# Keys of the first batch on a second DMA queue: windowed attention followed by a leaky-ReLU layer

## The chip, the cores and the metric

The kernel runs on one core of a Trainium2 chip. The metric is device time in microseconds, as the median of several runs. The core has five engines with instruction streams of their own, which meet only at semaphores: TensorE (PE, matrix products; loading its weights is listed as PEld), VectorE (DVE), ScalarE (ACT), GpSimd (POOL) and SyncE (SP). Memory transfers are done by 16 DMA engines. An engine that issues a transfer puts it into its queue and goes on; here SP and POOL issue transfers.

## The reference

Attention with a window of 32 positions on each side, over 8 batches, 8 heads, 576 positions and 64 channels, and after it two matrix products with a leaky ReLU between them:

```python
scores = scale * np.matmul(q, k.transpose(0, 1, 3, 2))
mask = np.abs(pos[:, None] - pos[None, :]) <= 32
scores = np.where(mask, scores, -1e9)
attn = softmax(scores)                      # over the last axis
attn_out = np.matmul(attn, v)
x = attn_out.transpose(0, 2, 1, 3).reshape(4608, 512)
h = x @ w_in                                # 512 -> 2048
out = np.maximum(0.01 * h, h) @ w_out       # 2048 -> 512
```

All inputs and the output are float32; the kernel computes in bfloat16 with float32 sums.

## The kernel before

Heads are handled in pairs (`p` from 0 to 3), so that two heads of 64 channels fill 128 partitions. A step of the attention is one half of the positions (288) of one pair of one batch; there are 64 of them. Step `i` has four parts. `score` (L270) multiplies keys and queries into `ps`, takes the exponential on ACT into `e` (L280), and multiplies it by a 0/1 mask on POOL into `prob` (L282). `sums` (L295) forms the row sums with a matrix of ones and their reciprocal on DVE (L309). `product` (L312) multiplies by the values into `x`. `scaled` (L332) multiplies `x` by the reciprocals into `xT` (L334). When the four pairs of a half are done, `h_tile` (L360, matmuls at L348) and `o_tile` (L381, matmuls at L390) do the dense layers for these 288 positions, and ACT applies the leaky ReLU (L355).

The order of the instructions is written out by hand and each engine takes its own in that order. The change lies in the opening, before a steady mixture of attention steps and dense matmuls begins.

The opening does this. At the top SP issues the loads of batch 0 in this order: queries and keys of pair 0, of pair 1, values of pair 0 (two halves, L91), queries and keys of pairs 2 and 3 (L79), values of pairs 1 to 3. A query or key load is 96 partitions x 2 heads of 1536 bytes each, 288 KB; a half of a value load is 64 partitions x 9 runs of 256 bytes, 144 KB. Eight completion counters are handed round over these loads, so a ninth load is issued only when the first has landed.

Queries are cast to bfloat16 on DVE (the last pair's on ACT, L195), keys on POOL (L197). TensorE transposes both (L225), ACT copies the transposes out of the accumulators (L233 for queries, L239 for keys), and DVE places keys into `kbd` (L258), a tile that holds the two heads on the diagonal and zeros elsewhere. Values go into a similar tile, `vbd`: pair 0 by POOL (`cast_v`, L205), pairs 1 to 3 by ACT (L203). The zeros in `kbd` and `vbd` are written once at the beginning: `kbd[0]` by DVE (L134), `vbd[0]` for pairs 0 to 2 by ACT (`clear`, L125 to L129, called at L135 to L137) and for pair 3 by POOL (L158).

POOL's order in the opening matters below. After the masks: keys of pair 0, keys of pair 1, both value halves of pair 0, the masking of step 0, keys of pair 2, the masking of step 1, keys of pair 3, three of the four loads of `w_in` (L448, issued from POOL since these loads also convert the type), the masking of step 2, the fourth load of `w_in`, then further maskings with the four loads of `w_out` (L452) between them. TensorE's filler matmuls (`keep_busy`, L398) add nothing to the result.

DVE's order is: query casts of pairs 0 and 1, key placement of pair 0, of pair 1, query cast of pair 2, reciprocal of step 0, key placement of pair 2, `xT` of step 0, reciprocal of step 1, key placement of pair 3, reciprocal of step 2, and so on. `first_pair` (L456) emits the transposes of one pair's queries and keys and the key placement.

Of the kernel before, what the change touches and what calls it, by code (L numbers as in the profile page):

```python
# [16 lines left out]
def kernel(  # L17
# [14 lines left out]
    nc = tc.nc  # L32
# [30 lines left out]
    qf, kf, vf = {}, {}, {}  # L63
    RUN = S // 96
# [3 lines left out]
    def load_qk(b, p, behind=None):  # L68

        for into, src, name in ((qf, q, "qf"), (kf, k, "kf")):
            t = fload.tile([96, 2, RUN * D], FP32, name=f"{name}{p}")
            if behind is not None:
                behind.memset(t[0:1, 0, 0:1], 0.0)
                behind = None
            heads = src[b, 2 * p:2 * p + 2]
            if b < BY_DMA:
                nc.sync.dma_start(out=t, in_=heads.rearrange("a (p c) d -> p a (c d)", c=RUN))  # L79
            else:  # L80
                nc.sync.dma_start(
                    out=t.rearrange("p a (g e) -> p a g e", g=3),
                    in_=heads.rearrange("a (g p c) d -> p a g (c d)", g=3, c=2),
                )
            into[b, p] = t

    def load_v(b, p):
# [7 lines left out]
        vf[b, p] = t  # L95

    load_qk(0, 0)
    load_qk(0, 1)
    load_v(0, 0)
    load_qk(0, 2)  # L100
    load_qk(0, 3)
    for p in range(1, NPAIR):
# [18 lines left out]
    vbd = [const.tile([128, NPAIR, NB, 128], BF16, name=f"vbd{i}") for i in range(2)]  # L121
# [3 lines left out]
    def clear(t, p):  # L125
        flat = t[:, p].rearrange("p n j -> p (n j)")
        nc.scalar.activation(
            out=flat, in_=zero.to_broadcast([128, NB * 128]), func=AF.Copy,
        )  # L129
# [4 lines left out]
    nc.vector.memset(kbd[0], 0.0)  # L134
    clear(vbd[0], 0)  # L135
    clear(vbd[0], 1)
    clear(vbd[0], 2)  # L137

# [7 lines left out]
    for lo in (0, 64):  # L148
        w = win[lo:lo + 64]
        nc.gpsimd.affine_select(  # L150
            out=w, in_=w, compare_op=ALU.is_ge, fill=0.0,
# [3 lines left out]
            out=w, in_=w, compare_op=ALU.is_ge, fill=0.0,  # L155
# [5 lines left out]
    def make_mask(hf):  # L161
# [12 lines left out]
        out=ps[:, 512:512 + HALF], in_=zero.to_broadcast([128, HALF]), func=AF.Copy,  # L174
# [11 lines left out]
    def cast_qk(b, p, q_eng=None):  # L186
        for eng, src, dst in ((q_eng or nc.gpsimd, qf, qb), (nc.gpsimd, kf, kb)):
            if b < BY_DMA:
                parts = [(dst[:, p], src[b, p].rearrange("p a (c d) -> p c a d", d=D))]
            else:  # L190
                by_c = src[b, p].rearrange("p a (g c d) -> c p g a d", g=3, c=2)
                parts = [(dst[:, p, 3 * c:3 * c + 3], by_c[c]) for c in range(2)]
            for to, tok in parts:
                if eng is nc.scalar:
                    eng.activation(out=to, in_=tok, func=AF.Copy)  # L195
                else:
                    eng.tensor_copy(out=to, in_=tok)  # L197

    def cast_v(b, p, on_act=False):
        for a in range(2):  # L200
            r = slice(64 * a, 64 * a + 64)
            if on_act:
                nc.scalar.activation(out=vbd[b % 2][r, p, :, r], in_=vf[b, p][r], func=AF.Copy)  # L203
            else:
                nc.gpsimd.tensor_copy(out=vbd[b % 2][r, p, :, r], in_=vf[b, p][r])  # L205
# [42 lines left out]
    def place_keys():  # L248

        while landing and landing[0][0] <= state["done"]:  # L250
            unplaced.append(landing.pop(0)[1:])
        while unplaced:
            b, p, kT = unplaced.pop(0)
            for a in range(2):
                r = slice(64 * a, 64 * a + 64)
                to = kbd[b % 2][r, p, :, r]
                if b < BY_DMA:
                    nc.vector.tensor_copy(out=to, in_=kT[r].rearrange("p (n j) -> p n j", j=64))  # L258
                else:
                    nc.vector.tensor_copy(  # L260
                        out=to.rearrange("p n (m c) -> p n c m", c=2),
                        in_=kT[r].rearrange("p (c n m) -> p n c m", c=2, n=NB),
                    )
# [192 lines left out]
    def first_pair():  # L456
        next(first)
        next(first)
        place_keys()
# [2 lines left out]
    make_mask(0)  # L462
    cast_qk(0, 1, nc.vector)
    first_pair()
    first_pair()
    cast_v(0, 0)
    score(0)
# [112 lines left out]
    at, t = {}, 0.0  # L580
# [66 lines left out]
```

## Time and profile before

| | |
|---|---|
| median of 3 runs | 319.5 us (319.1 to 320.05) |
| span of the profiled execution, first to last instruction | 318.5 us |
| time of the profiled execution beside its span | not listed |
| granted TensorE clock, mean | 1.000 |
| PE busy | 303.2 us, 95% |
| DVE busy | 218.2 us, 69% |
| POOL busy | 191.6 us, 60% |
| ACT busy | 182.6 us, 57% |
| bytes moved by DMA | 49.46 MB, mean 155 GB/s |

The profile comes from one execution of the kernel. Times in it are counted in microseconds from the first instruction. Its page has the busy share of each engine, the span in 40 equal slices with a digit for each (9 is 90% busy or more), the chain of work that ended last, and groups of instructions by line. The trace behind it can be asked for a timeline (start, duration, engine, line, operation, result and source, shapes, and in brackets the idle time before it with what ended it), for the waits, and for the DMA queues in a window of time. In the queue views q1 holds what SP issues and q0 what POOL issues. `SPq` is SP's issuing of a transfer; a DMA's landing is when its completion is seen.

### The profile page before, as it was taken

How to read it: one execution, taken by the hardware profiler on the slowest of the kernel's cores; microseconds unless marked ns; L12 is line 12 of the kernel's file. 1: busy time of each engine (PE TensorE's matmuls, PEld its weight loads, DVE VectorE, ACT ScalarE, POOL GpSimd, SP SyncE). 2: the span in 40 equal slices, each digit the busy share in tenths (PEclk: the TensorE clock that was granted, in tenths of full speed). 3: DMA queues.
4: the chain of work that ended last, by engine and by line, in shares of the span. 5: the costliest groups of instructions: out<-in, count | busy, mean ns of one | idle time of the engine just before them, and what ended most of it. 6: DMA issues, size and time to landing. Idle time of an engine off the chain costs nothing.

```text
span 318.5 us, 6474 instructions
## 1 busy us (share of the span) xinstructions
PE 303.2 (95%) x2449; PEld 204.3 (64%) x2449; DVE 218.2 (69%) x259; ACT 182.6 (57%) x393; POOL 191.6 (60%) x251
## 2 busy tenths in 40 slices
PE   2679998999999999999999999999999999999996
PEld 1467774585765858576765858576665858576653
DVE  5678955869655997688755997688745988565100
ACT  7577698474652828374652828375552837464531
POOL 7798963974546866686546866586637866330000
PEclk9999999999999999999999999999999999999999
DMA  8999999997999995399735995399733430000101
GB/s 179 211 186 218 267 250 203 250 206 181 216 242 196 231 206 150 82 251 203 155 76 127 238 227 136 75 223 232 162 76 104 109 70 33 35 35 2 66 31 71
DMA packets 108400, 49.46 MB, mean 155 GB/s; under 512 B 68816, under 2 KB 103888, under 8 KB 108368
## 3 DMA queue, kind: packets, MB, share of 16 engines
q1 hardware_dynamic: 104144, 44.84, 66.8%
q0 software_dynamic: 4224, 4.19, 8.0%
q8 instruction: 19, 0.31, 0.4%
q14 instruction: 13, 0.11, 0.1%
HBM read 36.70 MB, written 9.44 MB: 145 GB/s over the span
## 4 chain that ended last, share of the span: by engine, by line
PE 89%; DMA 3%; DVE 2%; SPq 1%; POOL 1%; ACT 1%; issue 1%; DVEq 0%; ACTq 0%
PE mm L348 39%; PE mm L390 38%; PE x L320 5%; PE ps L275 4%; DMA kf<-in_k_dram 3%; PE s L301 2%; DVE r L309 2%; SPq L79 1%; POOL w_in_bf L448 1%; DVE xT L334 1%; PE tp L225 1%; PE s L304 1%; ACT vbd L203 0%; SPq L91 0%; POOL prob L282 0%
## 5 line engine op out<-in xcount | busy, mean ns | idle before, releaser
L309 DVE RECIPROCAL r<-s 128x288 f32<-128x288 f32 x64 | 125.2, 1956 | 56.5 <-PE s L301 53.3
L282 POOL TENSOR_TENSOR prob<-e,mask 128x576 bf16<-128x576 bf16 x64 | 81.5, 1274 | 87.8 <-ACT e L280 41.1
L348 PE MATMUL mm<-xT,w_in_bf 128*128 128x288 bf16 x1024 | 134.0, 286 | 0.3
L390 PE MATMUL mm<-w_out_bf,gT 128*128 128x512 bf16 (+2 forms) x592 | 130.4, 373 | 0.2 <-DMA w_out_bf<-in_moe_w_out_dram 0.2
L355 ACT ACTIVATE gT<-mm 128x288 bf16<-128x288 f32 x256 | 101.4, 412 | 24.8 <-PE mm L348 8.5
L348 PEld LDWEIGHTS <-w_in_bf 128*128 128x128 bf16 x1024 | 98.4, 98 | 24.8 <-issue 0.6
L390 PEld LDWEIGHTS <-gT 128*128 128x128 bf16 x592 | 56.3, 98 | 59.6 <-issue 0.3
L395 ACT ACTIVATE o_sb<-mm 128x512 f32<-128x512 f32 (+2 forms) x37 | 21.7, 586 | 92.0 <-PE mm L390 92.0
L280 ACT ACTIVATE e<-ps 128x576 bf16<-128x576 f32 x64 | 41.4, 648 | 9.4 <-PE ps L275 9.2
L197 POOL CAST kb<-kf 96x384 bf16<-96x384 f32 (+1 forms) x56 | 35.5, 656 | 4.6 <-DMA kf<-in_k_dram 4.6
L205 POOL CAST vbd<-vf 64x576 bf16<-64x576 f32 x50 | 34.5, 689 | 1.8 <-DMA vf<-in_v_dram 0.4
L334 DVE TENSOR_TENSOR xT<-x,r 128x288 bf16<-128x288 f32 x64 | 29.3, 458 | 8.2 <-PE x L320 1.2
L260 DVE COPY kbd<-kT 64x576 bf16<-64x576 bf16 x48 | 32.3, 672 | 0.3
L275 PE MATMUL ps<-qT,kbd 128*128 128x128 bf16 (+2 forms) x320 | 26.5, 215 | 1.8 <-DVE kbd L258 1.2
L275 PEld LDWEIGHTS <-kbd 128*128 128x128 bf16 x320 | 21.0, 100 | 10.6 <-DVE kbd L258 1.5
L320 PE MATMUL x<-prob,vbd 128*128 128x128 bf16 (+2 forms) x320 | 26.0, 213 | 1.3 <-ACT vbd L203 0.7
L197 POOL CAST qb<-qf 96x384 bf16<-96x384 f32 x48 | 24.5, 538 | 0.0
L320 PEld LDWEIGHTS <-vbd 128*128 128x128 bf16 x320 | 20.6, 99 | 3.9 <-ACT vbd L203 1.8
L292 DVE TENSOR_TENSOR both<-prob 128x288 bf16<-128x288 bf16 x52 | 19.7, 380 | 0.9
L301 PE MATMUL s<-both,ones_bd 128*128 128x288 bf16 x52 | 14.9, 286 | 0.0
L258 DVE COPY kbd<-kT 64x576 bf16<-64x576 bf16 x16 | 7.1, 444 | 8.7 <-ACT kT L239 8.6
L225 PE MATMUL tp<-ident,qb 96*128 96x96 bf16 x48 | 4.4, 243 | 6.2 <-DVE qb L197 6.2
(43 smaller groups left out, 86.6 us busy)
## 6 DMA issues: line engine op xcount, KB each, us to landing
qf<-in_q_dram SPq DMA_DIRECT2D x32, 288.0 KB, 4.5
kf<-in_k_dram SPq DMA_DIRECT2D x32, 288.0 KB, 5.0
vf<-in_v_dram SPq DMA_DIRECT2D x64, 144.0 KB, 4.2
out_dram<-o_sb SPq DMA_DIRECT2D x35, 256.0 KB, 3.6
w_in_bf<-in_moe_w_in_dram POOLq DMA_DIRECT2D x4, 512.0 KB, 8.6
w_out_bf<-in_moe_w_out_dram POOLq DMA_DIRECT2D x4, 512.0 KB, 16.8
qT<-qb SPq DMA_TRANSPOSE x24, 4.1
kT<-kb SPq DMA_TRANSPOSE x24, 3.2
```

The costliest lines, as they stand in the source:

```text
L197: eng.tensor_copy(out=to, in_=tok)
L205: nc.gpsimd.tensor_copy(out=vbd[b % 2][r, p, :, r], in_=vf[b, p][r])
L260: nc.vector.tensor_copy(out=to.rearrange("p n (m c) -> p n c m", c=2), in_=kT[r].rearrange("p (c n m) -> p n c m", c=2, n=NB),)
L275: nc.tensor.matmul(ps_v[:, n_, :, i0:i0 + n], kbd[b % 2][:, p, blk], by_c[:, :, hf * EVEN + i0:hf * EVEN + i0 + n], start=True, stop=True,)
L280: nc.scalar.activation(out=e, in_=ps[:, P0:P0 + 2 * HALF], func=AF.Exp, scale=scale)
L282: nc.gpsimd.tensor_mul(pr.rearrange("p n c i -> p (n c i)"), e, mask[hf].rearrange("p n c i -> p (n c i)"),)
L309: nc.vector.reciprocal(r, s)
L320: nc.tensor.matmul(x_v[:, :, i0:i0 + n], vbd[b % 2][:, p, blk, :], pr[:, n_, :, i0:i0 + n], start=(blk == parts[0][1]), stop=(blk == parts ...
L334: nc.vector.tensor_mul(place(i), x, r)
L348: nc.tensor.matmul(h[:, 0:HALF], w_in_bf[:, c, ts(f, 128)], xT[:, c, ds(g * HALF % RING, HALF)], start=(c == 0), stop=(c == DMC - 1),)
L355: nc.scalar.activation(out=gT[:, f, ds(g * HALF % RING, HALF)].rearrange("p (i c) -> p i c", c=2), in_=h[:, 0:HALF].rearrange("p (c i) -> ...
L390: nc.tensor.matmul(o[:, lo:hi], gT[:, f, ds(128 * j % RING, 128)], w_out_bf[:, f, lo:hi], start=(f == 0), stop=(f == FFC - 1),)
```

## The change

The key loads of batch 0, for all four pairs, are issued by ACT into its own queue; the queries and values stay on SP. ACT issues the four loads ahead of everything else in its stream, the loading of its function table included. The zero fill of `vbd[0]` for pair 2 is taken from ACT and given to DVE, which does it after the key placement of pair 0 and ahead of that of pair 1. Later batches are loaded as before.

```diff
             heads = src[b, 2 * p:2 * p + 2]
+            ring = nc.scalar if name == "kf" and b == 0 else nc.sync
             if b < BY_DMA:
-                nc.sync.dma_start(out=t, in_=heads.rearrange("a (p c) d -> p a (c d)", c=RUN))
+                ring.dma_start(out=t, in_=heads.rearrange("a (p c) d -> p a (c d)", c=RUN))
             else:
                 nc.sync.dma_start(
...
     nc.vector.memset(kbd[0], 0.0)
     clear(vbd[0], 0)
     clear(vbd[0], 1)
-    clear(vbd[0], 2)
...
     cast_qk(0, 1, nc.vector)
     first_pair()
+    nc.vector.memset(vbd[0][:, 2], 0.0)
     first_pair()
     cast_v(0, 0)
     score(0)
```

With the eight completion counters handed round in the order of the code, SP's loads of queries of pairs 2 and 3 now wait until the keys and the queries of pair 0 have landed, and the values of pairs 1 to 3 until the keys and queries of pair 1, the keys of pair 2, the first half of pair 0's values, the keys of pair 3 and the second half of pair 0's values have landed, one each in this order.

## The prediction

> **What bounds the kernel now.** I read the page's busy shares and its forty slices first, to see where TensorE (PE) isn't full. The slices are 8 us each.
>
> ```profile
> PE 303.2 (95%) x2449; PEld 204.3 (64%) x2449; DVE 218.2 (69%) x259; ACT 182.6 (57%) x393; POOL 191.6 (60%) x251
> PE   2679998999999999999999999999999999999996
> DMA  8999999997999995399735995399733430000101
> ```
>
> PE is full from the fourth slice on: busy windows give 17.47 us of the 17.6 between 26.4 and 44 us. So only the start can give or take much, and what the start gains or loses comes out at the end undiminished. The edit lies wholly in the start. The granted clock is 1.00 throughout, so the clock does not enter.
>
> Next the chain of waits, cut to the first 27 us (start, length, what ran):
>
> ```profile
> 5.83 9.66 DMA kf<-in_k_dram
> 15.54 0.82 POOL kb L197
> 16.36 2.35 POOL w_in_bf L448 x3
> 18.73 1.30 POOL prob L282
> 20.52 1.97 DVE r L309
> 23.91 1.88 DVE r L309
> 26.39 0.65 PE mm L348 x4
> ```
>
> The fourth pair's keys (kf of pair 3) hold POOL, which then issues three weight loads, then masks pair 2's probabilities; two reciprocals on DVE follow, and the dense matmuls begin at 26.39. On this reading alone, earlier keys look like a large gain. The timeline of POOL shows how much is really there:
>
> ```profile
> 8.55 0.82 POOL L197 CAST kb<-kf 96x768 bf16<-96x768 f32 x1 [1.49 <-DMA kf<-in_k_dram]
> 9.32 0.66 POOL L205 CAST vbd<-vf 64x576 bf16<-64x576 f32 x1
> 10.35 0.67 POOL L205 CAST vbd<-vf 64x576 bf16<-64x576 f32 x1 [0.37 <-DMA vf<-in_v_dram]
> 11.46 1.27 POOL L282 TENSOR_TENSOR prob<-e,mask 128x576 bf16<-128x576 bf16 x1 [0.44 <-ACT e L280]
> 12.73 1.09 POOL L197 CAST kb<-kf 96x768 bf16<-96x768 f32 x1
> 13.79 1.27 POOL L282 TENSOR_TENSOR prob<-e,mask 128x576 bf16<-128x576 bf16 x1
> 15.54 0.82 POOL L197 CAST kb<-kf 96x768 bf16<-96x768 f32 x1 [0.49 <-DMA kf<-in_k_dram]
> ```
>
> POOL waits for the last keys only 0.49 us: until 15.06 it was busy with the queue in front of them. That queue hangs on pair 0's values (two L205 casts) and on the first exponential. Call the start of the first masking P0, here 11.46. From P0 to pair 2's masking at 18.73 POOL has 6.78 us of work and 0.49 us of waiting.
>
> Last, the transfers. From issue to landing (the trace's DMA issues in narrow windows), landings are: q0 4.2, k0 5.2, q1 6.9, k1 8.4, v0 first half 9.0, second half 10.2, q2 11.4, k2 12.6, q3 13.9, k3 15.5 us. SP had issued k3 by 6.6. The transfers land one after another, in order of issue, one 288 KB load per (15.5 - 10.2) / 4 = 1.33 us: it is the data movement, not the issue, that they wait for. How two queues share the engines is seen where the weights' queue (q0) and SP's (q1) both have work. First SP's queue alone (9 to 13 us), then both, with query and key loads (33 to 42 us), then both with value loads (45 to 46.4 us):
>
> ```profile
> DMA packets 640, 0.91 MB, mean 228 GB/s; under 512 B 47, under 2 KB 640, under 8 KB 640
> ...
> DMA packets 1982, 2.40 MB, mean 267 GB/s; under 512 B 112, under 2 KB 1980, under 8 KB 1980
> q0 software_dynamic: 992, 0.98, 64.6%
> q1 hardware_dynamic: 988, 1.40, 50.4%
> ...
> DMA packets 424, 0.28 MB, mean 200 GB/s; under 512 B 203, under 2 KB 424, under 8 KB 424
> q0 software_dynamic: 213, 0.22, 91.3%
> q1 hardware_dynamic: 211, 0.06, 30.6%
> ```
>
> Two things matter: the packets alternate one for one (992 to 988, 213 to 211), whatever their size, and both queues together are at best 267/228 = 1.17 times as fast as one; with values, 200 GB/s against 178 GB/s of values alone (14 to 17.5 us) and 228 of keys alone, nothing is gained.
>
> **The change part by part.**
>
> *Four key loads from SP to ACT.* SP loses four issues of about 0.45 us, so q1 and pair 0's values are issued 0.45 to 1.1 us earlier. Since they wait for data movement, this is worth nothing by itself. What changes is who is in front of whom. Before, k2 and k3 stood behind v0 in one queue. Now they sit in a second queue from 2.6 us on, and alternate with v0. A 288 KB key load is 192 rows of 1536 B; v0 is 1152 rows of 256 B. One for one, k2 and k3 (384 packets) are through before v0 has had its 384th packet of 1152. So v0's second half lands behind two more loads: 10.2 + 2 x 1.33 = 12.8 us with no gain in rate. That is the upper bound. The lower: everything up to v0's end (2.06 MB) runs at 1.17 times the rate from the first packets at 2.0 us: 2.0 + 10.8 / 1.17 = 11.2 us. Nearest to v0 beside keys is the row with values in it, which shows no gain in rate, so I take a point three quarters of the way up, 12.4 us.
>
> P0 is then 12.4 + 0.15 (landing to start, as 10.2 to 10.35) + 0.67 (the cast) + 0.04 = 13.26, 1.80 later than 11.46. Queued behind that cast on POOL are all the masking, kb of pairs 2 and 3 and the weight loads. The wait for k3 goes: 0.49 back. Sum on the chain: +1.80 - 0.49 = +1.3 us; with the bounds, 12.8 gives +1.7 and 11.2 gives P0 = 12.06 and +0.1.
>
> The first keys: k0 moves beside q0 and k1 beside q1, the same 1.15 MB, so k1 lands near 8.4 as before. q1's cast (DVE) and k1's (POOL) now fall together and TensorE takes the queries' transposes first, about 0.5 us: the first exponential is then ready near 11.9 instead of 11.32, still under 13.26. It is the next limit if v0 is early.
>
> Late next to it: q2 lands behind v0 at 12.4 + 1.33 = 13.7 (11.4 before). Its cast on DVE takes 1.39, to 15.1; the first reciprocal, ready at 13.26 + 1.27 + 0.7 = 15.2, doesn't wait for it. From there DVE has 1.96 + 0.85 + 0.46 + 1.95 + 0.91 = 6.1 us, to 21.4, before pair 2's reciprocal, which POOL sets at 20.52 + 1.3 = 21.8. So POOL stays the limit, by 0.4 us. q3 lands at 15.1 against 13.9 and ACT casts it at 15.13 today, hidden. Pair 0 to 3's other queue slots: SP's q2 and q3 now wait until k0 and q0 land (completion counters are reused after eight loads), about 5.2 us, long before their turn at 12.4. v1 to v3 land by 19.8 now and are first used at 18.81, 21.49 and 23.58; v1's 15.9 and 16.8 leave room for a load's time.
>
> *ACT's instruction stream.* ACT issues four loads first: 4 x 0.45 = 1.8 us ahead of the table load, minus one fill of 3.27 / 3 = 1.09 us: L173 ends near 6.6 instead of 5.88. Behind it queues L233, which starts at 6.42 after 0.55 us of waiting for TensorE, so some 0.2 us late; by L239 of pair 1, which waits 1.22 us for TensorE, nothing remains. If an issue on ACT cost twice SP's, L173 would end at 8.4, four evacuations of 0.65 follow, and the exponential would end near 11.7: still hidden by v0.
>
> *The fill on DVE.* The 128x2304 uint32 fill takes 1.98 us, a quarter of it 0.5. It stands between the two key placements, where DVE idles 2.12 us for ACT. Cost nothing; without that cover 0.5 us. Beside it POOL's casts could stretch (0.82 alone, 1.09 beside a DVE cast): 0 to 0.3 us, in idle time before v0.
>
> *Later stages.* The weights' first landing, 16.31 + 5.5 = 21.8, is needed at 23.50, and both move with POOL. The load stream behind it moves as a whole, so the 0.2 us that PE waits for the last w_out chunk near 48.8 stays.
>
> The sum: span 318.5 + 1.3 = 319.8. The page lists no time beside the span; the median of the runs, 319.5, is 1.0 above the span, and I keep that: 320.8 us.
>
> The Trainium skill ("DMA: Bandwidth & Descriptors", Issuing engines are not separate DMA queues) speaks against the change: a second issuing engine saves only issue time, since all run on the same 16 DMA engines. By that alone the sum is zero, 319.5. The same page (Queues, rings and completion order) lets each engine take turns between queues by the packet, of typically 9 to 17 descriptors; the rows above show single rows alternating, which is what makes the values late. Turns equal in bytes would put one key load in front of v0 rather than two.
>
> **The rivals.**
>
> *The two queues overlap well enough* (0.27). At 267/228 v0 lands at 11.2 and the sum is +0.1: 319.6, no change. Turns equal in bytes give 10.2 + 1.33 = 11.5 and +0.4, 319.9. For it: each queue alone is far under the 355 GB/s seen between 2.75 and 3.4 us. Against: the row with values.
>
> *Faster* (0.18): two queues hold the rate of that first burst, 355 GB/s. Then v0 lands near 2.0 + 2.06 / 0.355 + 1.5 (the spread between mean and last engine, from packets ending near 8.6 and the landing at 10.2) = 9.3, k1 near 6.8, and the exponential, about 3.5 us after k1, sets P0 near 10.3: -1.2 - 0.5 = -1.7, 317.8. It decides from P0 below 10.99, where 0.47 + 0.49 = 0.96 us is gained. Against: 258 GB/s is the mean from 2 to 6.5 us.
>
> *ACT is held by its issues* (0.05 within slower): needs above 1.2 us per issue, from where the exponential passes 13.26.
>
> **How the numbers follow.** Values late 0.50, held issues 0.05, overlap 0.27, faster 0.18. A measurement tells about 0.3% (0.96 us) from no change. The main case spans +0.1 to +1.7 (319.6 to 321.2); some of it is within 0.3%, and overlap gone a little wrong is slower, which I let cancel: faster 0.18, same 0.27, slower 0.55. The range cuts the fastest tenth and adds the fill and stretch (0.3 + 0.5) above: 318.3 to 321.9.
>
> **What would show it.** In the changed profile: v0's second cast on POOL starting near 12.5 with a wait on vf (today 10.35); no wait on kf before the last kb cast; pair 2's masking near 20.0 (18.73), the dense matmuls from about 27.7 (26.39); PE full after. Wrong if v0's cast starts by 11.3, if the first masking waits for the exponential instead, or if the start shifts and a later stage takes it back.

## The result and the profile after

The changed kernel takes 321.53 us (median of 4 runs, 320.95 to 323.05) against 319.3 us before (319.05 to 320.05): a ratio of 1.0078, 95% interval 1.0052 to 1.0103. By the medians it is 2.2 us slower, where 1.3 was forecast. The profiled execution took 321.19 us with a span of 319.5 us.

The page of the changed kernel, busy shares, the first of the forty slices (8 us each) and the queues:

```profile
PE 301.4 (94%) x2429; PEld 203.9 (64%) x2449; DVE 218.8 (68%) x260; ACT 181.3 (57%) x392; POOL 190.8 (60%) x251
PE   1579998999999999999999999999999999999996
...
q1 hardware_dynamic: 103312, 43.66, 64.1%
q0 software_dynamic: 4224, 4.19, 8.0%
q10 hardware_dynamic: 832, 1.18, 1.6%
```

TensorE's first three slices read 1, 5, 7 where they read 2, 6, 7 before; from the fourth on nothing is different. q10 is new: it holds what ACT issues. The chain of waits over the first 28 us, as start, length, what ran:

```profile
1.76 9.32 DMA vf<-in_v_dram
11.21 0.67 POOL vbd L205
11.93 0.68 POOL vbd L205
12.68 1.28 POOL prob L282
14.68 1.97 DVE r L309
18.98 0.66 ACT e L280
19.71 1.28 POOL prob L282
21.47 1.97 DVE r L309
27.35 0.30 PE mm L348
```

The keys are gone from its head and pair 0's values have taken their place: issued at 1.76, first half seen at 11.1. POOL's timeline shows what they hold up:

```profile
7.88 0.82 POOL L197 CAST kb<-kf 96x768 bf16<-96x768 f32 x1 [0.54 <-DMA kf<-in_k_dram]
11.21 1.39 POOL L205 CAST vbd<-vf 64x576 bf16<-64x576 f32 x2 [2.51 <-DMA vf<-in_v_dram]
12.68 1.27 POOL L282 TENSOR_TENSOR prob<-e,mask 128x576 bf16<-128x576 bf16 x1
13.90 1.15 POOL L197 CAST kb<-kf 96x768 bf16<-96x768 f32 x1
15.01 1.27 POOL L282 TENSOR_TENSOR prob<-e,mask 128x576 bf16<-128x576 bf16 x1
16.23 0.81 POOL L197 CAST kb<-kf 96x768 bf16<-96x768 f32 x1
19.71 1.27 POOL L282 TENSOR_TENSOR prob<-e,mask 128x576 bf16<-128x576 bf16 x1 [0.30 <-ACT e L280]
```

POOL idles 2.51 us for the values. Pair 0's exponential had been ready since 10.00 + 0.65 = 10.65, and the keys of pairs 2 and 3, the loads that the change brings forward, are cast without a wait, but only when the queue reaches them at 13.90 and 16.23. The last masking in the list waits 0.30 us for ACT, not for POOL's own queue.

This profile is 1.0 us longer than the profile of before that the prediction used, though the medians differ by 2.2. The first question for the experiments was where the other 1.2 us are.

### The profile page after: what moved, and what is told of

Read it like the earlier page. It is cut to its first block, busy times and chain, and to the rows that moved or that the text cites. A ratio compares the mean times of both kernels' runs of the same rounds, so it can differ in the third digit from the quotient of the medians.

```text
span 319.5 us, 6454 instructions
## 1 busy us (share of the span) xinstructions
PE 301.4 (94%) x2429; PEld 203.9 (64%) x2449; DVE 218.8 (68%) x260; ACT 181.3 (57%) x392; POOL 190.8 (60%) x251
## 4 chain that ended last, share of the span: by engine, by line
PE 83%; DMA 8%; DVE 3%; POOL 2%; ACT 1%; issue 1%; SPq 0%; DVEq 0%; ACTq 0%; POOLq 0%
PE mm L390 37%; PE mm L348 34%; DMA kf<-in_k_dram 5%; PE x L320 4%; PE ps L275 4%; DMA vf<-in_v_dram 3%; DVE r L309 2%; PE s L301 2%; POOL prob L282 2%; PE s L304 1%; DVE xT L334 1%; ACT gT L355 0%; POOL vbd L205 0%; ACT vbd L203 0%; ACT e L280 0%
## 5 line engine op out<-in xcount | busy, mean ns | idle before, releaser
L390 PE MATMUL mm<-w_out_bf,gT 128*128 128x512 bf16 (+2 forms) x572 | 128.7, 373 | 1.1
L197 POOL CAST kb<-kf 96x384 bf16<-96x384 f32 (+1 forms) x56 | 34.8, 644 | 4.5 <-DMA kf<-in_k_dram 4.5
L275 PE MATMUL ps<-qT,kbd 128*128 128x128 bf16 (+2 forms) x320 | 26.5, 215 | 1.8 <-DVE kbd L258 1.2
L275 PEld LDWEIGHTS <-kbd 128*128 128x128 bf16 x320 | 21.0, 100 | 10.6 <-DVE kbd L258 1.5
```

The source lines that it names most:

```text
L275: nc.tensor.matmul(ps_v[:, n_, :, i0:i0 + n], kbd[b % 2][:, p, blk], by_c[:, :, hf * EVEN + i0:hf * EVEN + i0 + n], start=True, stop=True,)
L390: nc.tensor.matmul(o[:, lo:hi], gT[:, f, ds(128 * j % RING, 128)], w_out_bf[:, f, lo:hi], start=(f == 0), stop=(f == FFC - 1),)
```

## The experiments

Two theories were to be told apart, with some smaller ones. **Late values**: the keys of pairs 2 and 3, in a queue of their own, go ahead of pair 0's values; POOL stands and everything behind it shifts. **ACT's stream**: ACT issues four loads before its table load and fills, and its evacuations come late. Diffs are against the changed kernel unless they say otherwise. "P0" is the start of the first masking, as in the prediction.

**The changed kernel again** (no edit).

> The changed kernel once more, for a firmer interval: its profiled span is 1.0 us above that of before, while the medians differ by 2.2 us. If only the late values and what queues behind them cost time (theory 'late values'): pair 0's first value cast on POOL again starts near 11.2 us, the first masking near 12.7, the dense matmuls near 27.35, and every profile shows about +1.0 us at the start; the median difference then comes out between 1.0 and 1.7 us with more runs. If something of the two queues differs from execution to execution (theory 'scatter'): the difference stays above 2 us and this profile shows another place of loss, beyond 28 us.

Measured: 321.72 us (6 runs) against 319.31, ratio 1.0078 (1.0064 to 1.0092). Its profile has P0 at 12.99, pair 2's masking at 20.01 and the dense matmuls at 27.65, span 319.8. The loss in the profile is at the start again and nothing is lost beyond 28 us. The median difference did not come down to 1.0 to 1.7. So the start is the place, and this points to a start of before that is usually earlier than its first profile had it. The next run tests that.

**The kernel before, again** (before, no edit).

> The kernel before, for a second profile of it. In the fill-only kernel, whose loads are those of before, the first masking started at 10.96 us, pair 2's masking at 17.99 and the fourth group of dense matmuls at 25.63; in the profile of before that the prediction used, these stand at 11.46, 18.73 and 26.39. If that profile was a late execution: here the values are nearer 11.0, 18.0 and 25.6, POOL doesn't wait for the last keys, and the span is near 317.6. If it was an ordinary one and the fill matters: near 11.5, 18.7 and 26.4 again.

Measured: 319.35 us against 319.42, ratio 0.9998 (0.9984 to 1.0011), span 317.4. POOL's timeline in this second profile of the kernel before:

```profile
7.73 0.82 POOL L197 CAST kb<-kf 96x768 bf16<-96x768 f32 x1 [0.35 <-DMA kf<-in_k_dram]
8.62 1.39 POOL L205 CAST vbd<-vf 64x576 bf16<-64x576 f32 x2
10.64 1.27 POOL L282 TENSOR_TENSOR prob<-e,mask 128x576 bf16<-128x576 bf16 x1 [0.63 <-ACT e L280]
...
14.19 0.82 POOL L197 CAST kb<-kf 96x768 bf16<-96x768 f32 x1
...
17.66 1.27 POOL L282 TENSOR_TENSOR prob<-e,mask 128x576 bf16<-128x576 bf16 x1 [0.30 <-ACT e L280]
```

Here the values are cast back to back from 8.62, P0 is 10.64 and waits for the exponential, and the last keys are cast at 14.19 without any wait. The dense matmuls start at 25.30. The first profile of before was a late execution, by 0.8 us at P0 and 1.1 at the dense matmuls, and its wait of 0.49 us for the last keys is not there in this one. Against this profile the changed kernel is later by 2.04 us at P0 (12.68 to 10.64), 2.05 at pair 2's masking (19.71 to 17.66) and 2.05 at the dense matmuls (27.35 to 25.30), and its span is 2.1 us longer. That is about the difference of the medians.

**The order alone, on one queue** (against before):

```diff
     load_qk(0, 0)
     load_qk(0, 1)
+    load_qk(0, 2, only="k")
+    load_qk(0, 3, only="k")
     load_v(0, 0)
-    load_qk(0, 2)
-    load_qk(0, 3)
+    load_qk(0, 2, only="q")
+    load_qk(0, 3, only="q")
```

> The loads stay on SP's one queue, and ACT's stream is as before; only the order is changed, so that the keys of pairs 2 and 3 are in front of pair 0's values. Late values: the second half of these values lands near 12.8 us (10.2 before), the first masking starts near 13.5 and the kernel is 1.0 to 1.7 us slower than before. Rival 'ACT's stream': ACT issues nothing here, so no loss, within 0.3 us of before. Rival 'two queues disturb one another': one queue only, no loss either.

Measured: 321.2 us, ratio 1.006 (1.0039 to 1.0082). POOL's timeline of this kernel (its line numbers are 4 higher):

```profile
11.46 0.66 POOL L209 CAST vbd<-vf 64x576 bf16<-64x576 f32 x1 [2.44 <-DMA vf<-in_v_dram]
12.40 0.67 POOL L209 CAST vbd<-vf 64x576 bf16<-64x576 f32 x1 [0.28 <-DMA vf<-in_v_dram]
13.15 1.27 POOL L286 TENSOR_TENSOR prob<-e,mask 128x576 bf16<-128x576 bf16 x1
```

One queue, no issue on ACT, and about the same loss at the same place. The order of the loads suffices; ACT's issuing and a second queue are not needed for it. (From P0 to pair 2's masking at 19.93 this kernel takes 6.78 us; in that profile TensorE runs the transposes ahead of it in 0.45 us instead of 0.69, and POOL does not wait for the exponential.)

**Only the first two key loads on ACT:**

```diff
-            ring = nc.scalar if name == "kf" and b == 0 else nc.sync
+            ring = nc.scalar if name == "kf" and b == 0 and p < 2 else nc.sync
```

> Of the four key loads only those of pairs 0 and 1 go to ACT; those of pairs 2 and 3 are back behind pair 0's values on SP, the fill stays on DVE. Late values: these values land at 10.2 us or earlier as before, the first masking starts near 11.5, and the time is that of before within 0.6 us. ACT's stream: half of the issues, so half the loss, 0.5 to 1.1 us slower. Two queues disturb one another: the first 1.15 MB still run on two queues, so most of the loss stays, about 1 us or more.

Measured: 319.29 us (11 runs) against 319.31, ratio 0.9993 (0.998 to 1.0007). With pair 2's and 3's keys behind the values again, the loss is gone, two queues and two issues on ACT notwithstanding. First POOL's, then TensorE's timeline:

```profile
9.38 0.67 POOL L205 CAST vbd<-vf 64x576 bf16<-64x576 f32 x1 [0.28 <-DMA vf<-in_v_dram]
10.42 1.27 POOL L282 TENSOR_TENSOR prob<-e,mask 128x576 bf16<-128x576 bf16 x1 [0.38 <-ACT e L280]
...
17.45 1.27 POOL L282 TENSOR_TENSOR prob<-e,mask 128x576 bf16<-128x576 bf16 x1 [0.30 <-ACT e L280]
...
17.41 1.65 PE L402 MATMUL ps<-mask,ones_bd 128*128 128x224 bf16 x8 [0.35 <-ACT e L280]
18.86 0.69 PE L304 MATMUL s<-prob,ones_bd 128*128 128x288 bf16 x2
```

P0 is 0.2 us ahead of the second profile of before. In this execution it is lost again on TensorE: the eight fillers take 1.65 us (0.93 in that profile of before) and the sums behind them 0.69 (0.41), and the dense matmuls start at 25.60 instead of 25.30.

**One key load in front instead of two** (keys of pairs 0, 1 and 3 on ACT):

```diff
-            ring = nc.scalar if name == "kf" and b == 0 else nc.sync
+            ring = nc.scalar if name == "kf" and b == 0 and p != 2 else nc.sync
```

> Keys of pairs 0, 1 and 3 on ACT, those of pair 2 back on SP behind pair 0's values: one load in front of the values instead of two. Late values: these land about 1.1 us later than with none in front (9.3 us) and 1.1 earlier than with two (11.6), so near 10.4; the first masking starts near 11.8, against 10.4 with none and 12.8 with two, and the kernel is about half as much slower as the changed one, 0.7 to 1.3 us. ACT's stream: three issues of four, so three quarters of the loss, 1.5 us or more.

Measured: 319.99 us against 319.42, 0.6 us by the medians and 0.8 by the ratio of 1.0026 (1.0008 to 1.0043), and in POOL's timeline:

```profile
11.06 0.67 POOL L205 CAST vbd<-vf 64x576 bf16<-64x576 f32 x1 [0.19 <-DMA vf<-in_v_dram]
11.82 1.27 POOL L282 TENSOR_TENSOR prob<-e,mask 128x576 bf16<-128x576 bf16 x1
```

P0 is where it was expected, and the loss at the lower end of what was expected. P0 goes with the number of loads in front of the values: 10.37 to 10.96 us with none (five profiles, and 11.46 in the first one of before), 11.82 with one, 12.44 to 13.15 with two (four profiles). The loss follows it, and not the number of ACT's issues, of which there are three here.

**The queue, without moving the fill:**

```diff
     clear(vbd[0], 1)
+    clear(vbd[0], 2)
...
-    nc.vector.memset(vbd[0][:, 2], 0.0)
```

> All four key loads on ACT as in the change, but the fill of pair 2's values stays on ACT, so ACT's stream is 1.09 us longer at the start. Late values: ACT ends its fills near 7.7 us instead of 6.7, its later evacuations catch up before the values land near 11.6, and the time is that of the changed kernel within 0.5 us (about 321.6). ACT's stream as the cause: another 0.7 to 1.1 us slower than the changed kernel (322.3 or more).

Measured: 321.13 us against 319.42, ratio 1.0053 (1.0038 to 1.0068). ACT's timeline:

```profile
0.81 2.17 ACTq L80 DMA_DIRECT2D kf<-in_k_dram  x4
4.30 3.27 ACT L128 ACTIVATE vbd<-zero 128x1152 bf16<-128x1152 bf16 x3
7.47 0.39 ACT L174 ACTIVATE ps<-zero 128x288 f32<-128x288 bf16 x1
10.71 0.65 ACT L281 ACTIVATE e<-ps 128x576 bf16<-128x576 f32 x1 [0.65 <-PE ps L276]
```

ACT ends its fills 1.1 us later than in the change (7.86 against 6.72), the first exponential starts 0.7 us later (10.71 against 10.00), and the kernel is not slower than the changed one: P0 is 12.44 and still behind the values. ACT's stream is no cause here; the values hide it.

**The fill alone** (all loads on SP as before, fill on DVE):

```diff
-            ring = nc.scalar if name == "kf" and b == 0 else nc.sync
+            ring = nc.sync
```

> The loads are all on SP as before; only the zero fill is moved from ACT to DVE. All theories: the fill lies in DVE's idle time between the two key placements, ACT's first evacuation still waits for TensorE, so within 0.3 us of before. If the fill on DVE slows POOL's casts beside it, up to 0.3 us slower.

Measured: 319.68 us against 319.31, ratio 1.0012 (0.999 to 1.0033): no difference that these runs can tell.

**The value casts behind the first masking:**

```diff
-    cast_v(0, 0)
     score(0)
+    cast_v(0, 0)
```

> The changed kernel with POOL's casts of pair 0's values put behind the first masking, so that the late values no longer hold POOL's queue; the loads are as in the change. Late values holding POOL alone: the first masking starts near 10.8 us instead of 12.7 and most of the 2.2 us comes back (320 or less). Late values and, behind them, late queries: pair 2's queries still land near 13.0 us, DVE casts them ahead of the first reciprocal until 14.4, so that the reciprocal starts at 14.4 instead of 14.7 and only about 0.3 us comes back (about 321.2).

Measured: 320.22 us against 319.63, ratio 1.0035 (1.0022 to 1.0048). That is 0.6 us slower by the medians and 1.1 by the ratio, so more than half of the loss is back, less than the one reading expected and more than the other. The chain says what is left, in an execution that took 320.81 us, 0.6 above the median:

```profile
11.11 1.27 POOL prob L282
12.38 0.61 POOL vbd L205
13.04 0.68 POOL vbd L205
13.77 1.13 POOL kb L197
14.91 1.23 POOL prob L282
16.14 0.77 POOL kb L197
16.91 2.36 POOL w_in_bf L448 x3
19.28 1.30 POOL prob L282
```

POOL now works without a gap from the first masking to pair 2's, 8.17 us: the 6.78 of the prediction and the 1.39 of the two casts, which before ran ahead of P0, in time that POOL had to spare. P0 is 0.47 us later here than in the second profile of before, the stretch behind it 1.15 longer, and that makes up the 1.6 us by which pair 2's masking is later. The late queries of pair 2 were not the limit, against the second reading.

**Two tries at a faster kernel**, from the one with two key loads on ACT. Fillers do not enter the result.

```diff
-    keep_busy(ps, 0, 8)
+    keep_busy(ps, 0, 4)
     sums(2)
```

> The kernel with two key loads on ACT, with four filler matmuls instead of eight ahead of step 2's sums. There the first masking was 1 us earlier than in the profile of before but the dense matmuls began no earlier, since TensorE ran the fillers at half speed (1.65 us for eight) and they ended after pair 2's masking. If that is where the gain went: step 2's sums start up to 0.3 us earlier and the time is 0.2 to 0.4 us below that kernel's 319.3. If the fillers are needed to bring TensorE to full speed: no gain, or slower by up to 0.5 us.

Measured: 319.79 us against 319.42, ratio 1.0016 (0.9996 to 1.0036). Step 2's sums start at 18.72 instead of 18.86, but the eight fillers after them (into `mm`) take 1.70 us instead of 0.93, and the dense matmuls begin at 25.70 instead of 25.60. In this profile, and in no other here, the granted clock falls; a digit is a slice of 8 us:

```profile
PEclk9979999999999999999999999999999999999999
```

It is 0.50 from 21 to 23 us, where these fillers run, and 1.00 again from 24 us. Ten of the twelve runs of this kernel have a mean clock of 0.999 or more and are no faster, so the gain is missing without this too. What was expected started from a wrong reading: with two key loads on ACT the dense matmuls did begin earlier than in the first profile of before, at 25.60 against 26.39. They were late only against the second one.

```diff
     sums(1)
-    keep_busy(ps, 0, 3)
...
-    keep_busy(ps, 0, 8)
+    keep_busy(ps, 0, 11)
     sums(2)
```

> The kernel with two key loads on ACT, with three filler matmuls moved from in front of pair 3's query transposes to behind its key transposes. From the first masking to pair 2's masking every run so far with early keys takes 7.03 us, of which POOL waits 0.30 for the exponential of step 2, whose scores stand behind these fillers on TensorE. If that order sets the stretch: the exponential comes 0.5 us earlier, the stretch is 6.75 us and the time 0.3 us below the 319.3 of that kernel and of before. If TensorE is then at half speed longer: no gain, as with fewer fillers.

Measured: 319.38 us against 319.63, ratio 0.9996 (0.9984 to 1.0007). The stretch is 10.81 to 17.56, 6.75 us, as expected, so the order of these fillers did set it. (The 7.03 us did not hold for every run with early keys: the order alone on one queue took 6.78.) But TensorE reached its faster rate later: the eleven fillers took 1.94 us and step 2's sums began at 19.08, after the masking that they wait for had ended. The gain is not seen in the time. No version here beats the kernel before by more than its interval.

## Why the prediction came out as it did

*The place and the mechanism* were right, but for the turns of the two queues (below): pair 0's values late behind the keys of pairs 2 and 3, POOL standing in front of their cast, the shift carried whole to the end. The order-only kernel, the dose of none, one and two loads, and the return with two loads on ACT show it. That the shift is carried whole: span minus start of the fourth group of dense matmuls is 292.1 us in the first profile of before (318.5 - 26.39), in the second (317.4 - 25.30), after (319.5 - 27.35), and with the order alone (319.7 - 27.57).

*The landing of the values.* Forecast 12.4 us for the second half, measured 2.5 + 9.2 = 11.7. But the ordinary execution of before has it at 3.5 + 5.7 = 9.2 instead of the 10.2 used, so the shift of 2.5 us is slightly more than the 2.2 forecast. It is that of two whole loads with no gain in rate: after its values that execution lands a load about every 1.13 us ((13.7 - 9.2) / 4), two in 2.3. The gain of 1.17 that gave the lower bound was not there. Its 228 GB/s for one queue belongs to the late execution; in the second profile of before one queue moved 258 GB/s from 9 to 13 us, and both queues 268 from 32 to 41. The changed kernel and the kernel with the same order on one queue, from 2 to 10 us:

```profile
DMA packets 2103, 1.97 MB, mean 246 GB/s; under 512 B 966, under 2 KB 2103, under 8 KB 2103
...
DMA packets 2087, 1.97 MB, mean 246 GB/s; under 512 B 946, under 2 KB 2087, under 8 KB 2087
```

Two queues and one moved the same. This agrees with the Trainium skill ("DMA: Bandwidth & Descriptors", Issuing engines are not separate DMA queues), by which issuing from several engines saves only the time of issuing. The rival of overlapping queues falls by it.

*The turns* went otherwise than forecast. Pair 0's values (q1) and the keys of pairs 2 and 3 (q10) in the changed kernel, from 6.8 to 7.8, 7.8 to 9 and 9 to 10 us:

```profile
q10 hardware_dynamic: 143, 0.20, 88.0%
q1 hardware_dynamic: 168, 0.04, 26.6%
...
q10 hardware_dynamic: 126, 0.18, 81.9%
q1 hardware_dynamic: 243, 0.06, 35.2%
...
q1 hardware_dynamic: 458, 0.12, 69.2%
q10 hardware_dynamic: 88, 0.11, 52.4%
```

The rows alternate about one for one only in the first of these windows. By 10 us the values had some 870 of their 1152 rows through, with the last key rows still to come, so "k2 and k3 (384 packets) are through before v0 has had its 384th packet" did not come about. The landing was that of two loads in front all the same, because the last rows of the values went after the last of the keys: from 10 to 11 us q1 has 399 records and q10 has 4. Turns equal in bytes do not fit either: the keys moved 0.49 MB here and the values 0.22, and with one load in front P0 is 0.9 us earlier than in the changed kernel. The second queue did not simply go first. These counts add up 16 engines, which need not be at the same load at one time, so how one engine takes its turns is not shown. Nor was a kernel tried that issues the keys of pairs 2 and 3 from ACT behind the values.

*The credit for the last keys* was the term of the sum that was mis-sized: "The wait for k3 goes: 0.49 back". From P0 to pair 2's masking the first profile took 7.27 us, with that wait in it; the second profile of before takes 7.02 and the changed kernel 7.03, and in neither does POOL wait for the last keys. So 0.24 came back against the first profile, and nothing against the second. What stands in the way is the exponential of step 2, for which POOL waits 0.30 us in both, and which the sum put at nothing. In the first profile it ended at 17.75 + 0.65 = 18.40, so pair 2's masking, at 18.73, could have come only some 0.3 us earlier. "So POOL stays the limit, by 0.4 us" was said of DVE and held: DVE waits 0.36 us for pair 2's sums.

*The base.* The sum was made on a late execution, whose values had landed late already. Against that one, P0 is 1.22 us later (forecast 1.80) and 0.24 comes back (forecast 0.49), which makes 0.98 where +1.3 was forecast; the span is 319.5, forecast 319.8. That the two errors nearly cancel is luck. Against the second profile P0 is 2.04 us later and nothing comes back, and that is the loss the medians show. The 1.0 us kept for what lies around the span was too small as well: in each of the changed kernel's runs the time is 1.65 to 1.75 us above the span, so the first profile of before belongs to an execution of about 320.2 us, above the median of 319.5. This is why the time came out 0.7 us above the forecast though the span did not.

*ACT*: fills ending near 6.6 us, measured 6.33 + 0.39 = 6.72; four issues take 2.07 instead of 1.8; the first exponential ends at 10.65, earlier than the 11.9 allowed for. Hidden, as forecast. *The fill*: 0.54 us instead of 0.5, in DVE's idle time. *The signs*: the second value cast starts at 11.9 (near 12.5 forecast), behind the first without a wait; the 2.51 us wait for values stands before the first, at 11.21.

## What to carry to other kernels

Here a second queue took no time off loads that wait for data movement (246 GB/s with one queue and with two); it changed who is in front, and the values came last. Whether their small rows were the reason was not tested apart from the order. Read the first wait of each in-order queue, not only the head of the chain: the keys headed it here, but POOL had at most 0.3 us to gain from them and over 2 us to lose from the values in front. A wait that goes away gives back only what the next one leaves. Where a change of one microsecond in 320 is forecast from one profile, compare its time with the median first, and don't count on a wait that may belong to that execution.

## What the runs showed of the hardware

Landings in the opening differ by about 1 us between executions of one program: the keys of pair 1 were cast at 8.55 us in the first profile of before and at 7.73 in the second, the values' second half landed at 10.2 and 9.2.

TensorE's rate in the opening also differs, though in all profiles but that of the kernel with four fillers the granted clock reads 1.00 there. Five matmuls of step 3's scores (L275) take 0.66 us from 19.34 in the profile with two key loads on ACT:

```profile
19.34 0.66 PE L275 MATMUL ps<-qT,kbd 128*128 128x96 bf16 x5
```

and 0.40 from 19.23 in the second profile of before:

```profile
19.23 0.40 PE L275 MATMUL ps<-qT,kbd 128*128 128x96 bf16 x5
```

In the fill-only kernel matmuls of the same form were down to 0.45 us at 16.48 already. Where the clock did read 0.50, from 21 to 23 us with four fillers, eight fillers took 1.70 us; in the profile with two key loads on ACT eight took 1.65 from 17.41, at a clock that reads 1.00. The granted clock of a profile is thus no proof of the faster rate; the durations of equal rows show it. The Trainium skill ("TensorE: Matmul & The Clock Gate", Part 1: The HAM clock gate) has TensorE at half clock until it has been busy for a window that runs free of the kernel's start; the longer rows, and their end at another time in each execution, agree with that, but no run here shows the window itself. In the profiles of two kernels this took up the 0.2 to 0.3 us won on POOL; whether it did so in their other executions is not shown.
